# An attention kernel with a dense layer behind it: engines of the small operations from a table, q and k of the last five groups turned by DMA, the last output tile in three parts

## The chip, the core and the metric

The kernel runs on one core of one Trainium2 chip. A core has five engines that run side by side, each through its own queue in order: PE (TensorE, matrix products and transposes through an identity), DVE (VectorE), ACT (ScalarE), POOL (GpSimd) and SP (SyncE, which here issues every DMA). Sixteen DMA engines move the data. The metric is the device time in microseconds, from several runs of the same program; less is better.

## What is computed

Inputs are q, k and v of shape (8 batches, 8 heads, 576 tokens, 64), and two weights, 512x2048 and 2048x512. Cut to what matters:

```python
q_d, k_d, v_d = mean over 4 neighbouring tokens          # 144 tokens
out_d = softmax(q_d @ k_d.T / 8) @ v_d
out_up = np.repeat(out_d, 4, axis=2)
mask = np.abs(pos[:, None] - pos[None, :]) < 4
out_local = softmax(where(mask, q @ k.T / 8, -1e9)) @ v
x = (out_up + out_local) as (4608 tokens, 512)
h = x @ w_in
out = (h - np.tanh(h)) @ w_out
```

So attention is cheap (a band of seven tokens, and a pooled version), and the dense part is large: 4608 x 512 x 2048 twice.

## The kernel before

**An order planned ahead.** The body doesn't issue instructions; it hands operations to a small planner, `Program` (L16). Each operation names its engine, an estimated duration in ns, what it reads and writes, and a priority `pri` (a lower number goes first). `choice` (L56) gives several engines with a duration for each, and the planner takes the one that can start first. `order` (L62) plays the program through with these durations, a lag behind each engine (`LAT`) and an added margin `spare` (L244), which depends on the priority: from 120 on, and again from `LATER` on, steps that wait for another engine are planned later than they need be. The resulting order of each engine's queue is fixed; on the chip each instruction waits only for its own inputs.

**Units.** A pair `p` (0 to 31) is two heads of one batch; four pairs are a batch (NP = 4). A group `n` (0 to 15) is two pairs, the unit in which q and k are loaded. The dense part has 9 blocks of 512 tokens.

**q and k.** `load_qk(n)` (L344) loads q (i = 0) and k (i = 1) into `qkn`. `reorder(n, i)` (L450) casts and sorts them into `qr` (bf16), on the engines of `REORDER`: any of three for groups 0 and 1, from group 2 on DVE for q and POOL for k. `turn(n, i)` (L459) turns `qr`: nine transposes on PE (L479) into a PSUM bank, a copy that spreads the result into `qk` (L486; ACT or DVE in groups 0 and 1, ACT later), and two sums that pool four tokens into `qkd` (L496 and L501; DVE or POOL in groups 0 and 1, POOL later). A branch `n >= FI` that turns `qr` by a DMA transpose into v buffers 4 and 5 is in the code, but `FI` is 99 and there are 16 groups, so it doesn't run.

**v.** `load_v(p)` (L362) loads v into one of six buffers `vst`; `prep_v(p)` (L415) casts it into `vw` (POOL or ACT for the first four pairs, then POOL). The pooled v is made on PE by `pool_v` (L423, copied out by ACT) for groups 0 to 6, and from group 7 by a second load and sums on POOL (`load_v4`, `sum_v`).

**A pair.** `attention(p)` (L510): first scores s1 on PE (L533), exp on ACT (L568), mask on DVE (L572); then s2 (the last tile's scores and the pooled ones, L533 and L552), exps (L591, L594), mask (L598); then the outputs on PE (L609, L615), a reciprocal and the norm into `ln` on DVE (L624, L626). Up to pair 11 `ln` is turned on PE, the pooled rows are copied by ACT to `od` (L667), and DVE adds both into `xT` (L669). From pair 12 (`XOUT`) `ln` is turned by a DMA transpose that SP issues (L634), and DVE adds (L645). The loads of pair p wait until the DMA turn of pair p - 5 was issued (`AHEAD` = 5). From pair 12 (`MERGE`) s1 of the next pair is issued together with s2.

**The dense part.** `mm1(kb, fc)` (L679) does four matmuls (L692) into one of four PSUM banks `ps_hy`, tanh on ACT (L701) and the difference on DVE into `gT` (L704). `mm2(kb, i)` (L711) does the second product (L720), four matmuls at a time; after sixteen ACT copies the 128x512 tile to `y` (L731) and SP stores it (L734). All dense matmuls have priority 5000, so PE takes them when nothing of attention is ready; their ACT and DVE steps have -1. Blocks 2 to 8 are interleaved with the second product of the block before. Block `kb` needs x of every batch that its tokens lie in: blocks 0 to 6 end in batches 0 to 6, blocks 7 and 8 in batch 7.

**The start.** PE has nothing dense to do until batch 0 is through; the planner fills its gaps there with matmuls on a constant tile (L903). The weights are loaded and cast (L410) in the meantime.

**What sets the order around the change.** The main loop (L868) visits the pairs; in each it hands in the pooled v of a new group, the cast of v of pair p + 2, the pair's scores, and the reorders and turns of the coming group, before or after the pair's second half by `INNER`, `OUTER` and `EARLY`; then the loads of the next group. The planner keeps its own order by priority and readiness; the place in the loop decides which use of a shared buffer comes first.

Of the kernel before, what the change touches and what calls it, by code (L numbers as in the profile page):

```python
# [11 lines left out]
ALU = mybir.AluOpType  # L12
# [3 lines left out]
class Program:  # L16
# [10 lines left out]
    def __init__(self):  # L27
        self.ops = []
        self.alternatives = {}
        self.touch = []  # L30
        self.fresh = set()
        self.spare = lambda pri, eng, to: 0
        self.last_write = {}
        self.readers = {}

    def op(self, eng, ns, fn, reads=(), writes=(), pri=0):
        i = len(self.ops)
        deps = set()
        for key in reads:
            if key in self.last_write:  # L40
                deps.add(self.last_write[key])
        for key in writes:
            if key in self.last_write:
                deps.add(self.last_write[key])
            deps.update(self.readers.get(key, ()))
        for key in reads:
            self.readers.setdefault(key, set()).add(i)
        for key in writes:
            self.last_write[key] = i
            self.readers[key] = set()  # L50
        deps.discard(i)
        self.ops.append((eng, ns, fn, deps, pri))
        self.touch.append(set(reads) | set(writes))
        return i

# [99 lines left out]
def kernel(  # L155
# [9 lines left out]
    nc = tc.nc  # L165
# [83 lines left out]
    LATER = 180  # L249
# [59 lines left out]
    def slot_v(p):  # L309
        return p % 4 if p >= 2 * FI else p % NVST  # L310
# [4 lines left out]
    def load_v4(n):  # L315

        b, h0 = n // 2, 4 * (n % 2)
        base = v[b, h0]
        for i, (g0, m) in enumerate(((0, 128), (128, 16))):
            rows = bass.AP(tensor=base.tensor, offset=base.offset + 4 * D * g0,  # L320
                           ap=[[4 * D, m], [S * D, 4], [1, 4 * D]])
            to = v4[128 - m:128, i]
            load(650, lambda to=to, rows=rows: nc.sync.dma_start(out=to, in_=rows),
                 [("qkn", 2, i, y) for y in range(2)], (1800, 250)[i], -30,
                 [("fl", 2 * n - AHEAD)])

    def sum_v(n):

        w, pri = n % NVW, 20 * n - 1
        for i in range(2):  # L330
            pp = slice(96 * i, 128)
            t = v4[pp, i].rearrange("p h (a d) -> p h a d", d=D)
# [11 lines left out]
    def load_qk(n):  # L344

        b, h0, s = n // 2, 4 * (n % 2), slot_qk(n)
        for i, src in enumerate((q, k)):
            for y in range(2):
# [13 lines left out]
    def load_v(p):  # L362

        b, j, s = p // NP, p % NP, slot_v(p)
        t = vst[s]
        for i in range(2):
# [48 lines left out]
    def prep_v(p):  # L415
        s, w, jj = slot_v(p), (p // 2) % NVW, p % 2
        P.choice([(eng, ns, lambda fn=fn: fn(  # L417
            out=vw[w][:, 2 * jj:2 * jj + 2, :, 0:64], in_=vst[s]))
                  for eng, ns, fn in CAST_V[p >= NEARLY]],
# [3 lines left out]
    def pool_v(hb):  # L423

        w = hb % NVW
        pri = 20 * hb - 1
# [3 lines left out]
        def mm():  # L430
# [11 lines left out]
           reads=[key], writes=[("vd", w)], pri=pri)  # L442
# [7 lines left out]
    def reorder(n, i):  # L450
        s, sn = n % 2, slot_qk(n)
        dst = qr[s][:, i].rearrange("p a (x d) -> p x a d", d=D)
        srt = qkn[sn][:, i].rearrange("p x (a d) -> p x a d", d=D)
        P.choice([(eng, ns, lambda fn=fn: fn(out=dst, in_=srt))  # L454
                  for eng, ns, fn in REORDER[n >= 2][i]],
# [3 lines left out]
    def turn(n, i):  # L459

        s = n % 2
        ps, po, ts, ox = banks_of(2 * n + i)
        if n in (1, 2):
            ps, ts = po, ox
        pri, cold = 20 * n, (1.5 if n < 1 else 1.0)
        b16 = ps.rearrange("p n c -> p (n c)").bitcast(BF16)[:, 0:A6 * 128]
        if n >= FI:
            b16 = vst[4 + i].rearrange("p h t d -> p (h t d)").bitcast(BF16)[:, 0:A6 * 128]
# [16 lines left out]
        def copy(fn):  # L485
            fn(out=o.rearrange("p y (g a) -> p y g a", a=A6),  # L486
               in_=b16.rearrange("p (a g y) -> p y g a", a=A6, y=2))
        P.choice([(eng, ns, lambda fn=fn: copy(fn)) for eng, ns, fn in TURN[n >= 2]],
                 reads=ts, writes=[("qk", s, i)], pri=pri)


        four = o.rearrange("p y (g a) -> p y g a", a=4)
        adders = ADDERS[n >= 2]

        def add1(eng):
            eng.tensor_tensor(out=half, in0=four[:, :, :, 0:2],  # L496
                              in1=four[:, :, :, 2:4], op=ALU.add)

        def add2(eng):
            with nc.allow_low_precision("pooled q and k"):  # L500
                eng.tensor_tensor(out=qkd[s][:, i], in0=half[:, :, :, 0],  # L501
                                  in1=half[:, :, :, 1], op=ALU.add)
        P.choice([(name, n1, lambda eng=eng: add1(eng)) for name, n1, _, eng in adders],
                 reads=[("qk", s, i)], writes=["half"], pri=pri)
        P.choice([(name, n2, lambda eng=eng: add2(eng)) for name, _, n2, eng in adders],
                 reads=["half"], writes=[("qkd", s, i)], pri=pri)

    nexts = {}

    def attention(p):  # L510
# [6 lines left out]
        late = 25 if p < 2 else pri  # L517
# [36 lines left out]
        qks = [("qk", sq, i) for i in range(2)]  # L554
# [6 lines left out]
        qkds = [("qkd", sq, i) for i in range(2)]  # L561
        if p <= MERGE:
            op("PE", 420 * cold, s1, reads=qks, writes=ts, pri=pri)
# [6 lines left out]
           reads=ts, writes=[("E", se, 0)], pri=pri)  # L570
# [16 lines left out]
        else:  # L587
            op("PE", 380 * cold, s2, reads=qks + qkds, writes=ox if p >= MERGE else ts,
               pri=pri)
        sb = ox if p >= MERGE else ts  # L590
        op("ACT", 335, lambda: A.activation(  # L591
            out=e2v, in_=pb[:, :, 0:96], func=AF.Exp, scale=SCALE),
           reads=sb, writes=[("E", se, 1)], pri=pri)
        op("ACT", 655, lambda: A.activation(  # L594
            out=e3, in_=pb[:, :, 96:384], func=AF.Exp, scale=SCALE / 16.0),
           reads=sb, writes=[("E", se, 2)], pri=pri)
# [8 lines left out]
        def outs():  # L605
# [13 lines left out]
        P.fresh.add(len(P.ops))  # L619
        op("PE", 570 * cold, outs,  # L620
# [9 lines left out]
            op=ALU.mult), reads=ox + [("r", s)], writes=[("ln", sl)], pri=late)  # L630
# [28 lines left out]
        def back():  # L659
# [8 lines left out]
           reads=ox, writes=[("od", s)], pri=late)  # L668
# [4 lines left out]
           reads=ox + [("od", s)], writes=[("x", b, j)], pri=late)  # L673
# [5 lines left out]
    def mm1(kb, fc):  # L679
# [15 lines left out]
        for part in range(2):  # L695
# [4 lines left out]
               writes=[("hy", slot)] + old, pri=5000)  # L700
# [8 lines left out]
    yn = [0]  # L709

# [28 lines left out]
    def dense(kb):  # L739
# [13 lines left out]
        for i in range(16):  # L753
            if kb < NBLK:
                mm1(kb, i)
            mm2(kb - 1, i)
# [3 lines left out]
    XOUT, T_OUT, AHEAD = 12, 1600, 5  # L760
    MERGE, GV = 12, 7
    FI, T_IN, EARLY = 99, 2050, 12
    XADD = [("DVE", (800, 350), V)]
    ORDER, W_FIRST = "g0123", "0123g"
    INNER, OUTER = {4: [0], 5: [1]}, {3: [0, 1], 7: [0, 1]}
    W_LATE = [300, 1400, 0, 0]
    T_QK, T_V, T_W, W_PRI, NEARLY = 900, 780, 2750, 33, NP
# [3 lines left out]
              [("POOL", 790, GP.tensor_copy)]]  # L771
    any3 = [("DVE", 860, V.tensor_copy), ("ACT", 950, A.copy),
            ("POOL", 1350, GP.tensor_copy)]
    REORDER = [[any3, any3], [[("DVE", 1150, V.tensor_copy)], any3[2:3]]]
    TURN = [[("ACT", 1125, A.copy), ("DVE", 1250, V.tensor_copy)],
            [("ACT", 1125, A.copy)]]
    ADDERS = [[("DVE", 760, 440, V), ("POOL", 1190, 850, GP)],
              [("POOL", 1190, 880, GP)]]
# [6 lines left out]
    for i in range(2):  # L785
        def guards(i=i):
# [3 lines left out]
           writes=[("qk", i, a) for a in range(2)])  # L790
# [26 lines left out]
    for step in W_FIRST:  # L817
        if step == "g":
            load_qk(2)
            load_v(4)  # L820
# [47 lines left out]
    for p in range(NPAIR):  # L868
        n = p // 2
        if p % 2 == 0 and 1 < n < GV:  # L870
            pool_v(n)
        if p + 2 >= NP and p + 2 < NPAIR:
            prep_v(p + 2)
        if p >= 2:
            next(work[p])
        inner = INNER.get(p, [] if p < 2 * NP else [p % 2] if p < EARLY else
                          [0, 1] if p == EARLY else [1] if p % 2 == 0 else [])
        m = n + 1 + (p > EARLY)
        outer = OUTER.get(p, [0] if p > EARLY and p % 2 else [])
        for i in inner if n + 1 < NGRP else []:  # L880
            reorder(n + 1, i)
            turn(n + 1, i)
        next(work[p], None)
        for i in outer if m < NGRP else []:
            reorder(m, i)
            turn(m, i)
# [48 lines left out]
```

## Time and profile before

| | |
|---|---|
| median of 13 runs | 340.86 us (339.39 to 343.98) |
| the profiled execution: time | 340.86 us |
| its span, first to last instruction | 339.1 us |
| mean granted clock of TensorE | 0.995 |
| busy: DVE, ACT, POOL | 228.1, 199.8, 157.9 us |
| dense matmuls L692 and L720, each | 576 loads of weights |
| transposes of q and k, L479 | 288 loads of weights |
| DMA: bytes, mean rate | 57.51 MB, 170 GB/s |
| DMA turns of `ln` (L634) | 20; 3.1 us to landing, 1.25 us to issue |

Times are from one profiled execution; L12 is line 12 of the kernel. "Busy" for PE contains pipelined matmuls whose ends are modelled, so rates are read from start to start. Where a queue sat idle, the profile names what ended the wait; idle time of an engine that isn't the bottleneck costs nothing. The granted clock is the share of full speed at which TensorE was let run in a stretch, and the DMA share is the mean busy share of the sixteen DMA engines. It can pass 1, since packets overlap.

The first matmuls of block 0 run at 26.1 and 26.7 us, and without a break from 29.5 us on. The last x is written at 265.3 us.

### The profile page before, as it was taken

What the parts mean: (1) busy time and instruction counts of PE and PEld (TensorE: products, weight loads), DVE (VectorE), ACT (ScalarE), POOL (GpSimd) and SP (SyncE); (2) the same over time, 40 slices, a digit from 0 to 9 for tenths busy, and PEclk for the clock granted to TensorE, in tenths of its full rate; (3) what the DMA queues carried; (4) which work ended last, traced back from release to release, by engine and by line L of the source; (5) the groups of instructions that cost most, each with busy time, mean ns of one, the idle gap of its engine ahead of it and who ended that gap; (6) DMA issues with size and microseconds to landing.
All of it is one profiled execution on the core that took longest, in us unless ns stands there. A gap on an engine that the chain in (4) does not pass through costs nothing.

```text
span 339.1 us, 6802 instructions
## 1 busy us (share of the span) xinstructions
PE 322.7 (95%) x2578; PEld 168.4 (50%) x2624; DVE 228.1 (67%) x369; ACT 199.8 (59%) x334; POOL 157.9 (47%) x178
## 2 busy tenths in 40 slices
PE   6786999999999999999999999999999999999995
PEld 2462554655565555555554545454444444444442
DVE  4986697568977877887689988986666433343300
ACT  1564887678967865676575757576544434444411
POOL 7743786496884449687458666862000000000000
PEclk9997999999999999999999999999999999999999
DMA  6999999999712598895798599962212000100021
GB/s 221 259 386 286 284 366 307 292 293 303 210 42 18 136 239 234 219 244 154 193 239 226 151 245 160 261 141 76 73 43 76 31 31 33 62 31 33 31 90 64
DMA packets 84749, 57.51 MB, mean 170 GB/s; under 512 B 62638, under 2 KB 67822, under 8 KB 84718
## 3 DMA queue, kind: packets, MB, share of 16 engines
q1 hardware_dynamic: 84718, 57.09, 61.9%
q8 instruction: 20, 0.33, 0.4%
q14 instruction: 11, 0.09, 0.1%
HBM read 43.05 MB, written 9.44 MB: 155 GB/s over the span
## 4 chain that ended last, share of the span: by engine, by line
PE 83%; DVE 7%; issue 3%; SPq 2%; DMA 2%; POOL 1%; ACT 1%; ACTq 0%; POOLq 0%; DVEq 0%
PE ps_hy L720 35%; PE ps_hy L692 33%; PE ps_ts L479 4%; PE ps_ts L533 3%; PE ps_ox L609 3%; PE ps_ox L615 2%; DMA vst<-in_v_dram 2%; SPq L357 1%; DVE gT L704 1%; DVE ln L626 1%; DVE xT L645 1%; PE ps_ox L432 1%; DVE E L572 1%; DVE xT L669 1%; DVE qr L454 1%
## 5 line engine op out<-in xcount | busy, mean ns | idle before, releaser
L692 PE MATMUL ps_hy<-xT,w_in_sb 128*128 128x512 bf16 x547 | 143.4, 383 | 3.8 <-DVE xT L669 1.8
L720 PE MATMUL ps_hy<-w_out_sb,gT 128*128 128x512 bf16 x560 | 140.7, 379 | 1.2 <-issue 0.3
L704 DVE TENSOR_TENSOR gT<-ps_hy,uy 128x512 bf16<-128x512 f32 x144 | 95.9, 686 | 62.5 <-ACT uy L701 60.4
L701 ACT ACTIVATE uy<-ps_hy 128x512 f32<-128x512 f32 x144 | 83.4, 602 | 69.3 <-PE ps_hy L692 64.1
L720 PEld LDWEIGHTS <-gT 128*128 128x128 bf16 x576 | 54.1, 98 | 61.4
L692 PEld LDWEIGHTS <-w_in_sb 128*128 128x128 bf16 x576 | 53.2, 98 | 60.7 <-issue 5.3
L496 POOL TENSOR_TENSOR half<-qk 128x576 f32<-128x576 bf16 x28 | 34.8, 1243 | 29.8 <-ACT qk L486 21.6
L486 ACT COPY qk<-ps_ts 128x1152 bf16<-128x1152 bf16 x26 | 29.3, 1127 | 10.4 <-PE ps_ts L479 8.9
L626 DVE TENSOR_TENSOR ln<-ps_ox,r 128x896 bf16<-128x896 f32 x30 | 32.7, 1089 | 0.8
L731 ACT COPY uy<-ps_hy 128x512 f32<-128x512 f32 x36 | 21.2, 590 | 18.3 <-PE ps_hy L720 17.6
L568 ACT ACTIVATE E<-ps_ts 128x960 bf16<-128x960 f32 x30 | 29.2, 977 | 3.7 <-PE ps_ts L533 2.9
L454 POOL CAST qr<-qkn 128x1152 bf16<-128x1152 f32 x17 | 21.9, 1286 | 18.8 <-DMA qkn<-in_k_dram 18.4
L334 POOL TENSOR_TENSOR qkn<-qkn 128x512 f32<-128x512 f32 (+1 forms) x18 | 24.2, 1346 | 7.9 <-DMA qkn<-in_v_dram 7.1
L572 DVE TENSOR_TENSOR E<-E,mask 128x960 bf16<-128x960 bf16 x28 | 24.3, 867 | 5.0 <-ACT E L568 5.0
L417 POOL CAST vw<-vst 128x640 bf16<-128x640 f32 x32 | 25.0, 794 | 4.5 <-DMA vst<-in_v_dram 2.0
L645 DVE TENSOR_TENSOR xT<-lnT 128x480 bf16<-128x480 bf16 (+1 forms) x40 | 24.0, 617 | 0.0
L501 POOL TENSOR_TENSOR qkd<-half 128x288 bf16<-128x288 f32 x29 | 22.7, 784 | 2.7 <-DVE half L496 1.3
L479 PEld LDWEIGHTS <-qr 128*128 128x128 bf16 x288 | 18.5, 99 | 9.7 <-DVE qr L454 3.7
L479 PE MATMUL ps_ts<-ident,qr 128*128 128x128 bf16 x252 | 19.2, 222 | 2.0 <-DVE qr L454 1.9
L598 DVE TENSOR_TENSOR E<-E,mask 128x192 bf16<-128x192 bf16 x28 | 12.9, 461 | 10.5 <-ACT E L591 10.4
L609 PE MATMUL ps_ox<-vw,E 128*128 128x65 bf16 x300 | 18.2, 194 | 0.3 <-DVE E L598 0.3
L609 PEld LDWEIGHTS <-E 128*128 128x128 bf16 x300 | 15.3, 98 | 6.3 <-DVE E L598 0.4
(90 smaller groups left out, 251.8 us busy)
## 6 DMA issues: line engine op xcount, KB each, us to landing
vst<-in_v_dram SPq DMA_DIRECT2D x62, 160.0 KB, 5.2
qkn<-in_q_dram SPq DMA_DIRECT2D x32, 288.0 KB, 4.0
qkn<-in_k_dram SPq DMA_DIRECT2D x32, 288.0 KB, 4.9
out_dram<-uy SPq DMA_DIRECT2D x36, 256.0 KB, 2.1
qkn<-in_v_dram SPq DMA_DIRECT2D x9, 512.0 KB, 5.0
gT<-in_moe_w_in_dram SPq DMA_DIRECT2D x4, 1024.0 KB, 9.0
xT<-in_moe_w_out_dram SPq DMA_DIRECT2D x8, 256.0 KB, 4.1
gT<-in_moe_w_out_dram SPq DMA_DIRECT2D x2, 1024.0 KB, 9.6
```

The costliest lines, as they stand in the source:

```text
L479: T.transpose(b16[:, 128 * a:128 * a + 128], qr[s][:, i, a, :], ident)
L486: fn(out=o.rearrange("p y (g a) -> p y g a", a=A6), in_=b16.rearrange("p (a g y) -> p y g a", a=A6, y=2))
L496: eng.tensor_tensor(out=half, in0=four[:, :, :, 0:2], in1=four[:, :, :, 2:4], op=ALU.add)
L568: op("ACT", 980, lambda: A.activation(out=e1, in_=ps[:, :, 0:480], func=AF.Exp, scale=SCALE), reads=ts, writes=[("E", se, 0)], pri=pri)
L572: op("DVE", 900, lambda: V.tensor_tensor(out=e1, in0=e1, in1=mask[:, 0:480].unsqueeze(1).to_broadcast([128, 2, 480]), op=ALU.mult), reads= ...
L609: T.matmul(po[:, hh, 65 * t:65 * t + 65], E[se][:, c:c + 128], vw[w][:, 2 * jj + hh, t, :], start=True, stop=True)
L626: op("DVE", 1090, lambda: V.tensor_tensor(out=ln[sl].rearrange("p n (h d) -> p h n d", d=D), in0=blocks[:, :, :, 0:64], in1=r[s].unsqueeze ...
L645: up=up: eng.tensor_tensor(out=xo[:, QW * t0:QW * t0 + nt * n].rearrange("p (t g a) -> p t g a", t=nt, a=4), in0=lnT[sl][:, t0:t0 + nt, 0: ...
L692: T.matmul(ps_hy[slot], w_in_sb[:, dc, fc * 128:(fc + 1) * 128], xT[dc][:, kb * 512:kb * 512 + 512], start=(dc == 0), stop=(dc == N_DC - 1))
L701: op("ACT", 490, lambda: A.activation(out=u[us], in_=ps_hy[slot], func=AF.Tanh), reads=[("hy", slot)], writes=[("u", us)], pri=-1)
L704: op("DVE", 620, lambda: V.tensor_tensor(out=gT[g][:, fc, :], in0=ps_hy[slot], in1=u[us], op=ALU.subtract), reads=[("hy", slot), ("u", us) ...
L720: T.matmul(ps_hy[slot], gT[g][:, fc, ts * 128:ts * 128 + 128], w_out_sb[:, fc, :], start=(fc == 0), stop=(fc == N_FF - 1))
```

## The change

Five things, with one table or setting each:

1. For groups 0 to 5 and pairs 0 to 11 the engine of each step is given by a table with an entry for each: the cast of v (`CV`), the reorder (`RE`), the copy of the turned tile (`TU`) and the sums (`AD`). Some copies and sums are split into two halves, one for each pair of the group (`TS`, `AS`), which may go to different engines. From group 6 on the engines are as before.
2. Groups 11 to 15 (`FI` = 11) are turned by the DMA transpose of the existing branch; the copy then reads SBUF. v of pairs from 22 on has four buffers in place of six, as two receive the turned tiles.
3. The last output tile (`last_tile`) is made in columns 0-256, 256-384 and 384-512, each with its own matmuls, copy (ACT, ACT, DVE) and store.
4. Places and priorities: which pair's loop turns a group stands in (`PLACE`), when pooled v is handed in (`PV`), a priority of -2 for some steps of pairs 4 to 11 (`URG`), other priorities for the last steps of pairs 0 to 3 (`LATE`), which groups' turns use the other PSUM bank (`TB`).
5. `AHEAD` is 6 in place of 5, and `LATER` 160 in place of 180.

The rest (`put`, `has`) are assertions at build time and issue nothing. `SPARE`, `MERGE`, `XOUT` and the planner are as before.

```diff
@@ slot of v
-        return p % 4 if p >= 2 * FI else p % NVST
+        if p < 2 * FI:
+            return p % NVST
+        return (p - 2 * FI + 2 * (FI % 3 == 1)) % 4
...
@@ prep_v
-                  for eng, ns, fn in CAST_V[p >= NEARLY]],
+                  for eng, ns, fn in CAST_V[CV.get(p, 1)]],
...
@@ reorder
-                  for eng, ns, fn in REORDER[n >= 2][i]],
+                  for eng, ns, fn in REORDER[RE.get((n, i), 3 + i)]],
...
@@ turn
-        if n in (1, 2):
+        if (n, i) in TB:
             ps, ts = po, ox
...
+        both = [(slice(0, 2), (0, 1))]
+        each = [(slice(y, y + 1), (y,)) for y in range(2)]
+        parted = TS.get((n, i), 0)
+        for k, (ys, yy) in enumerate(each if parted else both):
+            table = (TURN_H[parted - 1][k] if parted else
+                     TURN[3 if n >= FI else TU.get((n, i), 1)])
+            P.choice([(eng, ns, lambda fn=fn, ys=ys: copy(fn, ys)) for eng, ns, fn in table],
+                     reads=ts, writes=[("qk", s, i, y) for y in yy],
+                     pri=URG.get("turn", {}).get(n, pri))
...
+    def last_tile(kb, ts):
...
+        for c0, c1, engs in ((0, 256, "A"), (256, 384, "A"), (384, 512, "V")):
...
+            for e in range(4):
+                fcs = range(4 * e, 4 * e + 4)
+                op("PE", (c1 - c0) * 1.7, lambda fcs=fcs, mm=mm: mm(fcs),
...
+            fn = A.copy if engs == "A" else V.tensor_copy
...
@@ dense
-            mm2(kb - 1, i)
+            if kb < NBLK or i < 12:
+                mm2(kb - 1, i)
+        if kb == NBLK:
+            last_tile(kb - 1, 3)
@@ settings
-    LATER = 180
+    LATER = 160
...
-    XOUT, T_OUT, AHEAD = 12, 1600, 5
+    XOUT, T_OUT, AHEAD = 12, 1600, 6
+    P_A, LATE = 5000, {0: 26, 1: 5, 2: 25, 3: 25}
-    FI, T_IN, EARLY = 99, 2050, 12
+    FI, T_IN = 11, 2050
...
-    INNER, OUTER = {4: [0], 5: [1]}, {3: [0, 1], 7: [0, 1]}
+    TB = {(1, 0), (1, 1), (2, 0), (3, 0)}
+    PV = {2: -1, 3: 0, 4: 1, 5: 0, 6: 0}
+    PLACE = {2: (2, 4), 3: (1, 3), 4: (4, 4), 5: (0, 2), 6: (2, 3), 7: (1, 1), 8: (0, 3)}
...
+    CV = {0: 0, 1: 0, 2: 3, 3: 1, 4: 1, 5: 0, 6: 0, 7: 3, 8: 1, 9: 0, 10: 2, 11: 1}
...
+    RE = {(0, 0): 4, (0, 1): 4, (1, 0): 4, (1, 1): 4, (2, 0): 1, (2, 1): 0, (3, 0): 3, (3,
+          1): 4, (4, 0): 3, (4, 1): 4, (5, 0): 1, (5, 1): 1}
     TURN = [[("ACT", 1125, A.copy), ("DVE", 1250, V.tensor_copy)],
-            [("ACT", 1125, A.copy)]]
+            [("ACT", 1125, A.copy)], [("DVE", 1250, V.tensor_copy)],
+            [("ACT", 2210, A.copy)]]
+    TU = {(0, 0): 0, (0, 1): 0, (1, 0): 1, (1, 1): 0, (2, 0): 0, (2, 1): 0, (3, 0): 0, (3,
+          1): 0, (4, 0): 2, (4, 1): 1, (5, 0): 2, (5, 1): 0}
...
+    TS, AS = {(0, 0): 1, (1, 1): 3, (4, 0): 3}, {(0, 1): 3, (1, 1): 3}
+    URG = {'e1': {4: -2, 5: -2, 6: -2, 7: -2}, 'od': {4: -2, 5: -2, 6: -2, 7: -2}, 'norm':
+          {8: -2, 9: -2, 10: -2, 11: -2}, 'add': {4: -2, 5: -2, 6: -2, 7: -2}, 'turn': {4:
+          -2, 5: -2}}
...
+    AD = {(0, 0): 0, (0, 1): 1, (1, 0): 0, (1, 1): 2, (2, 0): 1, (2, 1): 0, (3, 0): 0, (3,
+          1): 0, (4, 0): 1, (4, 1): 0, (5, 0): 0, (5, 1): 2}
```

In `CV`, `RE` and `TU` the numbers pick a row: of the v casts 0 is POOL or ACT, 1 POOL, 2 ACT, 3 DVE; of the reorders 0 is any of three, 1 DVE, 2 ACT, 3 DVE and 4 POOL with the durations of the later groups; of the copies 0 is ACT or DVE, 1 ACT, 2 DVE, 3 ACT from SBUF. In `AD` 0 is DVE or POOL, 1 POOL, 2 DVE.

## The prediction

> **What bounds the kernel.** First, the busy shares and the chain of waits (the work that ended last, followed back from the end):
>
> ```profile
> PE 322.7 (95%) x2578; PEld 168.4 (50%) x2624; DVE 228.1 (67%) x369; ACT 199.8 (59%) x334; POOL 157.9 (47%) x178
> PE 83%; DVE 7%; issue 3%; SPq 2%; DMA 2%; POOL 1%; ACT 1%; ACTq 0%; POOLq 0%; DVEq 0%
> ```
>
> PE carries the chain. A busy PE need not be an efficient one, so I look at what it does. The dense part is 1152 matmuls (9 blocks, 64 on L692 and 64 on L720), and a run of eight takes 1.73 us from start to start, 0.216 each: 248.8 us. Attention fills the gaps. So the end is: when the dense stream begins, plus all PE work after that, plus PE's idle time, plus the tail behind the last matmul. I take the stages in that order, by the table of busy time per stretch (columns: us, then busy us and instructions of PE, PEld, DVE, ACT, POOL, granted clock, DMA share, GB/s):
>
> ```profile
> 28.00:29.00 1.00, 0.28 (x6) 0.18 (x4) 0.32 (x1) 0.51 (x2) 0.20 (x1) 1.00 0.99 373
> 31.00:32.00 1.00, 1.00 (x4) 0.37 (x3) 0.94 (x3) 0.60 (x1) 0.00 (x0) 0.50 0.94 169
> ...
> 160.00:180.00 20.00, 19.75 (x176) 10.59 (x178) 15.20 (x27) 12.80 (x21) 10.75 (x12) 1.00 0.84 210
> 180.00:200.00 20.00, 19.33 (x169) 10.19 (x172) 18.66 (x28) 13.18 (x22) 15.20 (x16) 1.00 0.74 189
> 200.00:222.00 22.00, 21.84 (x180) 11.24 (x182) 19.50 (x28) 13.98 (x24) 14.96 (x15) 1.00 1.01 228
> 222.00:244.00 22.00, 21.84 (x185) 11.28 (x185) 16.55 (x29) 13.84 (x23) 7.90 (x8) 1.00 0.33 73
> ```
>
> Before 29.5 us PE waits for x; DVE, the engine that makes x, is the full one there (8.8 of 10 us in both 10-20 and 20-30). From 29.5 on PE hardly stops: 3.3 us idle in all of 30-240, 0.4 behind that. The clock is at half from 30 to 33, which costs some 1.7 us (15 matmuls in 4.9 us, not 3.2).
>
> **The supply of x is as tight as PE.** Blocks 7 and 8 run L692 and L720 in turn, 32 steps of 1.73 us, 55.3 us in all; L692 ends at 320.6, so block 7 starts at about 265.3. The timeline says when the last x is there (first line), and how far apart the pairs' second scores (s2) stand behind the last turn:
>
> ```profile
> 265.07 0.25 DVE L645 TENSOR_TENSOR xT<-lnT 128x96 bf16<-128x96 bf16 x1
> ...
> 235.66 0.21 PE L533 MATMUL ps_ox<-qk 64*128 64x96 bf16 x2
> ...
> 244.16 0.21 PE L533 MATMUL ps_ox<-qk 64*128 64x96 bf16 x2
> ...
> 253.29 0.22 PE L533 MATMUL ps_ox<-qk 64*128 64x96 bf16 x2
> ```
>
> Batch 7 becomes ready in the very microsecond in which PE wants it. Time taken off PE counts only if attention comes earlier too.
>
> **q and k of groups 11-15 turned by DMA.** Ten turns of nine transposes leave PE. One costs, from its start to that of what follows it:
>
> ```profile
> 208.80 0.67 PE L479 MATMUL ps_ts<-ident,qr 128*128 128x128 bf16 x9
> 209.30 1.89 PE L720 MATMUL ps_hy<-w_out_sb,gT 128*128 128x512 bf16 x8
> ```
>
> 0.50 us; ten are 5.0, on the path (the 0.67 is a modelled end that overlaps its successor). They come back elsewhere:
>
> - DMA. The nearest row is the turn of ln (128x896, 229 KB), issued at 243-245 with nothing else moving: shares of 0.62 and 0.57 in two stretches of 1 us, 1.2 us of all engines. Scaled by 1152/896 a turn of q or k is 1.5, ten are 15. The Trainium skill (DMA: Bandwidth & Descriptors, Latency and other measured facts) gives DMA transposes 261 GB/s where the middle dimension isn't contiguous: 1.1 each for 295 KB, 11 in all. The row decides. From 162 to 222 DMA is busy for 0.90 x 60 = 54 us; with 15 it is 69, 9 us more than fit. Cover: the last turn is at 225.5 and its user is the score of pair 30 at 243.9, or 238.9 when PE runs 5 us ahead: 13 us. So hidden, with 4 us to spare. If the landing time (3.1 us of the ln turns) were the cost, 31 us: the third rival.
> - SP. An issue took 1.25 us, so 12.5 us in a queue that also issues loads, ln turns and outputs, and each stands behind the reorder it waits for: DVE for q, POOL for k. Behind it in the queue stand the next loads. AHEAD 6 instead of 5 lets those go one pair (about 8 us) sooner, more than a wait for one reorder (1.3 us). Nothing taken.
> - v buffers fall from six to four behind pair 22. A load then waits for the cast of the pair four before; that cast stands two pairs ahead of its own pair, so it is done when the load may go by AHEAD anyway. Nothing.
> - ACT. The copy that spreads the turned tile now reads SBUF. The row that it has from PSUM:
>
> ```profile
> L486 ACT COPY qk<-ps_ts 128x1152 bf16<-128x1152 bf16 x26 | 29.3, 1127 | 10.4 <-PE ps_ts L479 8.9
> ```
>
> The copy reads with a step of 128 elements (256 bytes). The skill's page SBUF — State Buffer (Door 1: The DMA port swizzle) says that each access that crosses into another 16-byte line pays a penalty; the diff's table prices the copy at 2.21. No row here shows it. By the row ten copies cost nothing new; by the rule and the table some 11 us more. ACT has 40.0 busy in 160-222, so 51 of 62 us: it fits, but tanh and exp sometimes stand behind a 2.2 us copy. I take the dearer.
>
> New waits: the fullest engine of before, DVE in 180-200 (93%), goes with 0.67 us of idle PE per 20 us. Were ACT to do the same over 62 us, 2.1 us, against 1.08 idle there now: +1.0. Bounds: 0 (ps_hy has four slots) and 3.3, as much as all the idle of 30-240 again.
>
> **The tables for batches 0-2.** From 30 to 120 PE is idle for 1.6 us in all, so there they can hardly bring time, only let x come sooner or later. Before 29.5 they can. On DVE they remove the reorder of q 0 (0.76), half of two copies (1.36 each: 1.36) and perhaps the copy of k 0 (1.35); they add one v cast (estimate 0.55, from 0.42 for 512 columns on DVE). Net 1.6 to 2.9 less, in a chain where DVE is full but for the 0.6 us before 19.4, when it waited for the first output. Against it: all four reorders stand on POOL (1.15 each), where the mask of 1.90 lies at 5.3; k 0 can come 1.15 later. Bounds +1.2 and -2.9; I take -1.5, as the v casts (12.84 at the earliest, when v landed) hold part of the chain. The cold clock I leave: the gap ahead of 29.5 gets shorter, not closed.
>
> **The last tile in parts.** Behind the last matmul:
>
> ```profile
> 335.53 0.59 ACT L731 COPY uy<-ps_hy 128x512 f32<-128x512 f32 x1 [2.87 <-PE ps_hy L720]
> 336.15 0.33 SPq L734 DMA_DIRECT2D out_dram<-uy  x1
> ```
>
> The copy of 128 columns costs a quarter of the elements: an estimate of 0.25 from the 128x96 row above, 0.34 less. The last transfer is a quarter too: 262 KB took 0.7 of a microsecond (share 0.70 in 245-246), so some 0.5 less. PE: 32 matmuls of 128 columns at 0.056 (nine in 0.50) and 16 of 256 at 0.108, 3.5 us for 3.46. Sum -0.8; bounds 0 (fixed cost of a DMA is all) and -1.2.
>
> **Sum.** -5.0 + 1.0 - 1.5 - 0.8 = -6.3. The profiled execution's span was 339.1 and its time 340.86, the median too, so 1.76 lies around the span: 332.8 + 1.76 = **334.6**.
>
> **Rivals.**
>
> - Supply sets the end (attention no faster). For it: pairs behind the last turn stand 8.5 and 9.1 us apart with no turn between, as far as those with turns (187.5 to 195.9, 8.4), so the turns do not pace the chain of a pair. Against: loads go out earlier, the score bank is held by no turn (1.8 us and more each) from group 11 on, and what batches 0-2 gain is lead. Then only front and tail count: -2.3, **338.6**.
> - More goes: the clock stays up at 30-33 (1.7) and half of the idle PE of 30-240 (1.6) goes: 334.6 - 3.3 = **331.3**. For it: the gap before the stream may fall under what drops the clock; against: PE still waits for DVE there.
> - DMA becomes the bound (slower). Place: 160-240, where the share is 0.74 to 1.01 already. At 3.1 us a turn, 54 + 31 = 85 us of transfers in 60, 25 late, 13 covered: 12 us late, **346.6**. It makes the kernel slower than before from 2.63 us a turn (6 free + 13 covered + 7.3, by ten). Against: the share at 243-245 says 1.2 for a tile nearly as large.
>
> That the change does not do what it says shows as L479 with 288 loads of weights, not 198; nothing in the diff speaks for it.
>
> **Chances and range.** Forecast 0.54, supply 0.20, more 0.12, DMA 0.14. What a measurement can tell from no change is 0.3%, 1.0 us. Faster: the first three, less 0.05 of the supply case near 340: 0.81. Same 0.05, slower 0.14. The forecast's own range, from the new waits (0 to 3.3), the front (1.2 to -2.9) and the tail, each seldom at its end, is 332 to 337.5; to leave out two in ten it takes in the supply case and part of the better one: 330.8 to 339.3.
>
> **What would show it.** Right: L479 at 198 weight loads; span about 333; last x near 259; start of the steady L692 near 28. ACT's copies from SBUF near 2.2 us, PE idle in 160-222 near 2. Wrong: last x still at 264-265 and PE idle or out of dense work before it (supply); qk copies waiting for the DMA turns with shares of 1 past 222 (DMA); a first L692 stream at 29.5 or later (front).

## The result and the profile after

The changed kernel takes 337.81 us in the median of its 11 runs (335.19 to 339.51), against 340.92 for the kernel before, beside it and in the runs shown earlier (48 in all). The ratio is 0.9905, interval 0.9878 to 0.9932: faster by 3.1 us, where 6.3 were forecast. The profiled execution took 337.05, its span was 335.3, so 3.8 below the profiled one of before. One later execution of `turns_only`, at a granted clock of 0.558 from end to end, took 553.42 us and is left out everywhere; six other executions lie over 1.5% above the fastest of their kernel and stay in, as they move no median in the table below by more than 0.3 us.

The page of the changed kernel (busy us, share of the span, instructions; then groups with the mean ns of one):

```profile
PE 319.3 (95%) x2522; PEld 165.5 (49%) x2565; DVE 239.4 (71%) x385; ACT 207.7 (62%) x337; POOL 150.7 (45%) x168
...
L514 ACT COPY qk<-ps_ts 128x1152 bf16<-128x1152 bf16 (+1 forms) x15 | 16.0, 1064 | 13.9 <-DVE qk L514 8.1
...
L514 ACT COPY qk<-vst 128x1152 bf16<-128x1152 bf16 x10 | 22.2, 2221 | 1.6 <-POOL half L518 1.6
```

PE is as full as before, with 56 instructions fewer (90 transposes less, 32 small matmuls more, a few records missing). The ten copies that now read SBUF (from `vst`) take 2.22 us each where the same copy from PSUM takes 1.13: the table in the diff was right, and the dearer end was the one to take.

The busy time by stretch, in the columns of the prediction's table. The first four rows are the stretches shown there for before. The last four are two earlier stretches, each of the changed kernel and then of before:

```profile
160.00:180.00 20.00, 19.63 (x153) 9.60 (x156) 16.47 (x25) 15.28 (x23) 11.92 (x13) 1.00 1.05 235
180.00:200.00 20.00, 19.89 (x153) 9.65 (x148) 15.88 (x27) 17.58 (x25) 14.45 (x16) 1.00 1.19 234
200.00:222.00 22.00, 21.84 (x185) 10.98 (x186) 20.17 (x32) 16.19 (x25) 13.96 (x14) 1.00 1.08 230
222.00:244.00 22.00, 21.84 (x170) 10.81 (x169) 16.64 (x29) 15.40 (x23) 8.27 (x8) 1.00 0.42 107
...
40.00:70.00 30.00, 28.11 (x274) 15.81 (x277) 26.90 (x40) 20.66 (x36) 18.84 (x22) 1.00 1.00 308
40.00:70.00 30.00, 29.38 (x295) 16.57 (x298) 23.41 (x36) 22.56 (x39) 20.68 (x25) 1.00 1.04 318
70.00:120.00 50.00, 48.97 (x489) 27.50 (x497) 43.99 (x68) 38.55 (x66) 31.82 (x33) 1.00 0.68 174
70.00:120.00 50.00, 49.07 (x482) 27.67 (x489) 40.47 (x65) 39.61 (x66) 34.73 (x37) 1.00 0.60 164
```

From 160 to 222 PE is idle for 0.64 us (1.08 before), although ACT rose from 40.0 to 49.1 us and the DMA share from 0.87 to 1.11. The late half, where the large gain was to come from, does somewhat better than forecast. The early half doesn't: in 40-70 PE is idle for 1.9 us where it was 0.6. The timeline of PE says when the dense stream begins and when PE gets the last x of batch 2, first in the changed kernel and then before (in brackets the idle time before an entry, and what ended it):

```profile
29.26 6.75 PE L739 MATMUL ps_hy<-xT,w_in_sb 128*128 128x512 bf16 x23 [1.21 <-DVE xT L715]
...
102.96 0.72 PE L453 MATMUL ps_ox<-vw,pick 128*128 128x256 bf16 x5 [0.34 <-DVE xT L715]
...
29.49 5.08 PE L692 MATMUL ps_hy<-xT,w_in_sb 128*128 128x512 bf16 x15 [1.21 <-DVE xT L669]
...
101.03 0.72 PE L432 MATMUL ps_ox<-vw,pick 128*128 128x256 bf16 x5 [0.34 <-DVE xT L669]
```

The stream begins 0.2 us sooner than before, not 1.5, and x of batch 2 is complete at 102.9, where it was 101.0. From there to the last matmul it is 102.9 to 332.4, 229.5 us, against 101.0 to 335.45, 234.45 us: 4.95 less. That this meets the 5.0 of the turns is partly chance, for the other tables and settings are in it too; `fi99` below takes the turns off alone. So this pair of profiles reads: 1.9 us lost in front of batch 3, 5.0 won behind it, and at the end

```profile
328.69 3.70 PE L769 MATMUL ps_hy<-w_out_sb,gT 128*128 128x256 bf16 x48
...
332.48 0.29 DVE L777 COPY uy<-ps_hy 128x128 f32<-128x128 f32 x1 [13.49 <-PE ps_hy L769]
```

2.9 us of tail behind the last matmul instead of 3.65. Sum: 1.9 - 5.0 - 0.7 = -3.8.

**Equal clocks.** A profile is one execution, and the spans of one and the same kernel differ by up to 5 us. Each run lists its mean granted clock, and the spread goes with it. In the profiles the clock falls to a half for 3.4 us or a multiple of it: from 30.0 to 33.4 us before, and from 8.7 to 12.1 and 29.2 to 32.6 in the changed kernel. I call 3.4 us of this a cold stretch. Each takes 0.005 off the mean (half of 3.4, in 337), so a mean of 0.99 stands for two. Among 78 runs of the kernel before, the median span is 337.9 with no cold stretch (0.998 or more, 27 runs), 338.7 with one (21), 339.9 with two (0.988 to 0.992, 11) and 340.9 with three (19): about 1 us for each, less than the 1.7 that the prediction worked out for the one at 30.

So the table gives, beside medians, the median span at full clock (0.998 or more) and with two cold stretches, each with its number of runs. The changed kernel was run again beside the last experiments and has 18 runs in all, of which 14 have two. Like with like the change is worth 4.3 us (full clock) or 3.9 us (two cold stretches); the medians show 3.1, because it is seldom at full clock.

| kernel | median time, us | span at full clock (runs) | with two cold stretches (runs) |
|---|---|---|---|
| before (78 runs) | 340.62 | 337.9 (27) | 339.9 (11) |
| changed (18) | 337.47 | 333.6 (2) | 336.0 (14) |
| `fi99`: changed, no DMA turns | 341.57 | 338.5 (4) | 340.6 (5) |
| `whole`: changed, last tile whole | 338.34 | 334.8 (4) | 337.6 (6) |
| `tables_old`: changed, old tables | 337.74 | 335.1 (3) | none |
| `turns_only`, `turns_2`: before, DMA turns | 338.42 | 335.6 (7) | 336.6 (4) |
| `front_new`: before, new tables of groups 0, 1 | 345.37 | 340.4 (2) | 342.4 (1) |
| `front_old`: changed, those tables old | 339.73 | 336.0 (2) | 338.3 (6) |
| `ahead5`: changed, AHEAD 5 | 339.79 | 334.7 (2) | 338.2 (6) |
| `old_lead`: `tables_old`, LATER 999 | 337.67 | 334.8 (3) | 335.8 (2) |
| `warm`, `warm_2`: changed, six fillers | 335.42 | 333.2 (6) | 338.2 (2) |

Runs of one kernel at full clock still spread by 1 to 3 us, so differences under 1 us say little, and a median of two or three runs says little more. Behind 40 us and up to the last matmul the clock is full in every profile but that of the execution left out, so stretches of two profiles can be compared there directly.

### The profile page after: what moved, and what is told of

It reads as the page before. It is cut to its first block, busy times and chain, and to the rows that moved or that the text cites. A ratio compares the mean times of both kernels' runs of the same rounds, so it can differ in the third digit from the quotient of the medians.

```text
span 335.3 us, 6713 instructions
## 1 busy us (share of the span) xinstructions
PE 319.3 (95%) x2522; PEld 165.5 (49%) x2565; DVE 239.4 (71%) x385; ACT 207.7 (62%) x337; POOL 150.7 (45%) x168
## 4 chain that ended last, share of the span: by engine, by line
PE 77%; SPq 7%; DVE 6%; DMA 6%; issue 2%; ACT 1%; POOL 0%; POOLq 0%; DVEq 0%; ACTq 0%
PE ps_hy L739 32%; PE ps_hy L794 32%; DMA qkn<-in_k_dram 5%; SPq L398 3%; PE ps_ox L652 3%; PE ps_ts L572 2%; SPq L372 2%; PE ps_ox L658 2%; PE ps_ts L505 2%; DMA xT<-in_moe_w_out_dram 1%; DVE gT L751 1%; PE ps_hy L769 1%; DVE ln L671 1%; SPq L417 1%; SPq L410 1%
## 5 line engine op out<-in xcount | busy, mean ns | idle before, releaser
L739 PE MATMUL ps_hy<-xT,w_in_sb 128*128 128x512 bf16 x549 | 143.1, 383 | 4.3 <-DVE xT L715 2.2
L794 PE MATMUL ps_hy<-w_out_sb,gT 128*128 128x512 bf16 x545 | 137.5, 379 | 0.8 <-issue 0.2
L739 PEld LDWEIGHTS <-w_in_sb 128*128 128x128 bf16 x576 | 53.5, 98 | 62.5 <-issue 5.2
L794 PEld LDWEIGHTS <-gT 128*128 128x128 bf16 x560 | 52.6, 98 | 59.1
L518 POOL TENSOR_TENSOR half<-qk 128x576 f32<-128x576 bf16 x26 | 31.8, 1221 | 50.1 <-ACT qk L514 44.5
L805 ACT COPY uy<-ps_hy 128x512 f32<-128x512 f32 x35 | 20.9, 597 | 14.9 <-PE ps_hy L794 13.2
L348 POOL TENSOR_TENSOR qkn<-qkn 128x512 f32<-128x512 f32 (+1 forms) x18 | 24.9, 1385 | 7.2 <-DMA qkn<-in_v_dram 5.6
L691 DVE TENSOR_TENSOR xT<-lnT 128x480 bf16<-128x480 bf16 (+1 forms) x40 | 26.5, 676 | 0.0
L477 POOL CAST qr<-qkn 128x1152 bf16<-128x1152 f32 x17 | 21.1, 1243 | 8.6 <-DMA qkn<-in_k_dram 8.0
L514 ACT COPY qk<-ps_ts 128x1152 bf16<-128x1152 bf16 (+1 forms) x15 | 16.0, 1064 | 13.9 <-DVE qk L514 8.1
L514 ACT COPY qk<-vst 128x1152 bf16<-128x1152 bf16 x10 | 22.2, 2221 | 1.6 <-POOL half L518 1.6
L634 ACT ACTIVATE E<-ps_ox 128x192 bf16<-128x192 f32 x20 | 6.7, 334 | 18.6 <-PE ps_ox L591 17.4
L572 PEld LDWEIGHTS <-qk 64*128 64x128 bf16 x320 | 9.3, 95 | 16.2 <-issue 13.8
```

The costliest lines, as they stand in the source:

```text
L348: op("POOL", 1330, lambda t=t: GP.tensor_tensor(out=t[:, :, 0:2], in0=t[:, :, 0:2], in1=t[:, :, 2:4], op=ALU.add), writes=keys, pri=pri)
L514: fn(out=o[:, ys].rearrange("p y (g a) -> p y g a", a=A6), in_=b16.rearrange("p (a g y) -> p y g a", a=A6, y=2)[:, ys])
L518: eng.tensor_tensor(out=half[:, ys], in0=four[:, ys, :, 0:2], in1=four[:, ys, :, 2:4], op=ALU.add)
L691: up=up: eng.tensor_tensor(out=xo[:, QW * t0:QW * t0 + nt * n].rearrange("p (t g a) -> p t g a", t=nt, a=4), in0=lnT[sl][:, t0:t0 + nt, 0: ...
L739: T.matmul(ps_hy[slot], w_in_sb[:, dc, fc * 128:(fc + 1) * 128], xT[dc][:, kb * 512:kb * 512 + 512], start=(dc == 0), stop=(dc == N_DC - 1))
L794: T.matmul(ps_hy[slot], gT[g][:, fc, ts * 128:ts * 128 + 128], w_out_sb[:, fc, :], start=(fc == 0), stop=(fc == N_FF - 1))
```

## The experiments

Each part of the change can be taken off alone. The old tables are put back as values of the new ones; together with FI 99, AHEAD 5, LATER 180 and the whole tile that is the kernel before, instruction for instruction, so no part of the change is left out. Theory A and theory B in the expectations are two readings of the first result, told in the first of them.

### The parts alone

`tables_old`:

```diff
-    CV = {0: 0, 1: 0, 2: 3, ...}
+    CV = {p: 0 for p in range(4)}
-    RE, TU, AD = (a table of groups 0-5 each)
+    RE, TU, AD = 0 for groups 0 and 1
-    TS, AS, URG = {(0, 0): 1, ...}, ...
+    TS, AS, URG = {}, {}, {}
-    PV, PLACE, TB, LATE = (as changed)
+    PV, PLACE, TB, LATE = (as before)
```

> The changed kernel with every table and place of batches 0-2 as before (engines of casts, reorders, copies and sums, no halves, no priorities of -2); DMA turns, last tile, AHEAD 6 and LATER 160 stay. Theory A (the tables cost some 1.9 us, since x of batch 2 is there at 102.9 instead of 101.0; the DMA turns give their 5.0 us in full): 5.7 us below before, about 335.2, x of batch 2 near 101, PE idle in 40-70 back to 0.6 us from 1.9. Theory B (the tables do nothing, the DMA turns give only half because x of batch 7 comes no sooner): as the changed kernel, 337.5, x of batch 7 at 264-265.

Neither. 337.74 is the changed kernel's time. The early loss is gone, as theory A has it: x of batch 2 comes at 100.5 (in a profile without a cold stretch), and PE is idle for 1.0 us in 40-70. But from there to the last matmul it takes 231.7 us, where the changed kernel takes 229.5; its PE is idle for 2.1 us in 200-330 (0.7 before, 1.0 changed). Whether the new tables pay once the DMA turns are in is not settled: at full clock the old ones are 1.5 us slower (3 runs against 2), in the medians 0.3, and `old_lead` below, with the old tables too, is level with the changed kernel at two cold stretches.

`fi99`:

```diff
-    FI, T_IN = 11, 2050
+    FI, T_IN = 99, 2050
```

> The changed kernel with no group turned by DMA (FI 99), everything else as changed. Theory A: 5.0 us above the changed kernel, about 1.2 above before, 342. Theory B: 2.5 above the changed kernel, about 340.

341.57, ratio to before 1.0014 (0.9979 to 1.0049). The profile of `fi99` is the cleanest measure of the turns, for it has its two cold stretches within half a microsecond of where the changed kernel has them. PE gets the last x of batch 2 at the same time; here are that point and the last matmuls, first of `fi99`, then of the changed kernel:

```profile
102.89 0.72 PE L453 MATMUL ps_ox<-vw,pick 128*128 128x256 bf16 x5 [0.34 <-DVE xT L715]
...
333.77 2.93 PE L769 MATMUL ps_hy<-w_out_sb,gT 128*128 128x256 bf16 x41
...
330.83 1.56 PE L769 MATMUL ps_hy<-w_out_sb,gT 128*128 128x128 bf16 x25
```

336.7 against 332.4: 4.3 us behind batch 2. At full clock it is 4.9, with two cold stretches 4.6: theory A's term. (The 4.1 between the medians mixes clocks, and most runs of `fi99` have 2.0 us or more around the span, where the others have 1.7.) The rest of the change on its own gains nothing, though the tile in it is worth about 1.

`whole`:

```diff
-            if kb < NBLK or i < 12:
-                mm2(kb - 1, i)
-        if kb == NBLK:
-            last_tile(kb - 1, 3)
+            mm2(kb - 1, i)
```

> The changed kernel with the last tile in one piece as before. Both theories: 0.75 us above the changed kernel, with 3.65 us from the last matmul to the end of the span instead of 2.9.

338.34, 0.9 above the changed kernel in the median, 1.2 at full clock; in its profile 4.0 us stand behind the last matmul, 1.1 more than in the changed one. The forecast for the tile was 0.8. That profile also says that the late x of batch 2 is not the clock's doing: it has one cold stretch (29.4 to 32.8 us), as before has, and is 2.2 us behind before all the same:

```profile
103.22 0.72 PE L453 MATMUL ps_ox<-vw,pick 128*128 128x256 bf16 x5 [0.34 <-DVE xT L715]
```

`turns_only`, and `turns_2`, the same kernel once more:

```diff
 (the kernel before)
-    FI, T_IN, EARLY = 99, 2050, 12
+    FI, T_IN, EARLY = 11, 2050, 12
```

> The kernel before with FI 11 alone (AHEAD 5, LATER 180, last tile whole). Theory A: 5.0 us below before, 336. Theory B: 2.3 below before, 338.6. If AHEAD 6 is what lets the turns pay: 1 to 2 us slower than tables_old after the 0.75 of the tile, with DMA-fed copies late and PE idle in 160-222 above 2 us.

> The kernel before with FI 11 alone, once more, for a profile at a normal clock. Theory D (old tables and AHEAD 5 leave PE short of work once the turns are gone): span 2.4 us below before at full clock, idle PE from 120 on 2 us above the 1.7 of before, and copies of turned tiles or dense matmuls of a new block named as late. Rival: no more idle PE than before and the 2.4 us was noise of three runs; then it is 4.5 to 5 below.

338.42 in 21 runs, 335.6 at full clock: 2.3 below before (3.3 with two cold stretches, and 3.7 by the profiles behind batch 2: 230.8 us against 234.5). The turns are worth 2.3 to 3.7 us in the kernel before and 4.3 to 4.9 in the changed one. The profile of `turns_2` shows a part of the difference. Its row of 200-240, then that of before, and ACT and PE around the last turned tiles:

```profile
200.00:240.00 40.00, 38.21 (x307) 18.99 (x311) 31.34 (x51) 32.92 (x47) 24.59 (x26) 1.00 0.85 205
200.00:240.00 40.00, 39.68 (x341) 20.83 (x346) 32.48 (x51) 26.23 (x43) 22.86 (x22) 1.00 0.73 162
```

```profile
230.86 4.29 ACT L514 COPY qk<-vst 128x1152 bf16<-128x1152 bf16 x2
235.02 0.61 ACT L805 COPY uy<-ps_hy 128x512 f32<-128x512 f32 x1
235.49 0.63 ACT L748 ACTIVATE uy<-ps_hy 128x512 f32<-128x512 f32 x1
```

```profile
235.20 0.38 PE L572 MATMUL ps_ts<-qk 64*128 64x120 bf16 x8 [0.58 <-ACT qk L514]
236.90 1.45 PE L739 MATMUL ps_hy<-xT,w_in_sb 128*128 128x512 bf16 x6 [0.18 <-DVE gT L751]
```

PE is idle for 1.8 us in 200-240, 0.3 before. Two copies of 2.2 us stand one behind the other on ACT; a dense output copy and a tanh wait behind them for four microseconds, and PE waits for the scores and then for the free bank. In the changed kernel the ten copies are 3.5 us or more apart from start to start, and PE's idle time in 200-240 is 0.3. From 120 on the idle PE of `turns_2` is 3.4 us against 2.1 before (to 330): 1.3 us of what is missing are seen as waits; the rest could not be placed. Copies that meet are not the whole cause. In `tables_old` they are 3.5 us or more apart too, and yet its PE is idle for 3.4 us from 120 to 330, 1.5 of it in three waits for output copies (L805), at 137, 203 and 267.

### Is it the supply of x?

`old_lead`:

```diff
 (tables_old)
-    LATER = 160
+    LATER = 999
```

> The old tables with DMA turns, last tile and AHEAD 6 (as in tables_old, whose span at full clock was 335.1, with 2.1 us of idle PE in 200-330), and the second step of margin off (LATER 999), so that late pairs are planned closer together. Theory D (with old tables the DMA turns are held back by the supply of x): x of batch 7 earlier by 2 us or more, idle PE in 200-330 under 1 us, span at full clock near 333.6. Rival (PE's idle there comes from waits that the margin prevents): as slow or slower, more idle PE.

x of batch 7 came at 263.3, where it was 264.1 in `tables_old`: 0.8 us sooner, not the 2 that were wanted. Idle PE in 200-330 went from 2.1 to 1.6 us, but rose from 1.3 to 1.8 in 120-200, and the time is the same (334.8 at full clock, three runs from 333.3 to 336.5). So this run hardly tests theory D; `turns_2` speaks more against it, for its x of batch 7 is the earliest of all (262.5) and its PE is no less idle.

`ahead5`:

```diff
-    XOUT, T_OUT, AHEAD = 12, 1600, 6
+    XOUT, T_OUT, AHEAD = 12, 1600, 5
```

> The changed kernel with AHEAD 5. If the earlier loads carry the DMA turns: copies of turned tiles late, PE idle in 160-240 from 0.8 to above 1.8 us, 1 us or more slower (334.6 at full clock and above). If they don't matter: within 0.5 us of the changed kernel.

339.79: 2.3 us slower in the median, 1.1 at full clock (2 runs), 2.2 with two cold stretches (6 runs). So AHEAD 6 is worth 1 to 2 us here, where the prediction had it at nothing. Its profile, full in clock from 35 us on, shows a part of the way. Behind batch 2 it takes 231.1 us (229.5), and two of the copies meet on ACT, as in `turns_2`. The row is to be read beside the changed kernel's 21.84 of 22:

```profile
222.00:244.00 22.00, 20.98 (x161) 10.18 (x163) 17.00 (x27) 18.34 (x26) 12.57 (x14) 1.00 0.76 185
...
237.30 4.29 ACT L514 COPY qk<-vst 128x1152 bf16<-128x1152 bf16 x2
...
243.35 1.89 PE L739 MATMUL ps_hy<-xT,w_in_sb 128*128 128x512 bf16 x8 [0.61 <-DVE gT L751]
```

PE is idle for 1.0 us there, 0.2 in the changed kernel. Whether AHEAD 6 would pay as much without DMA turns, no run says; with the old tables it does not show (231.7 us behind batch 2 in `tables_old` with AHEAD 6 and LATER 160, 230.8 in `turns_2` with 5 and 180).

### The front

`front_old` (the changed kernel, with the tables of groups 0 and 1, pairs 0-3 and LATE as before):

> The changed kernel with the tables of groups 0 and 1 and pairs 0-3 (and their priorities) as before; those of groups 2-5 as changed. If the new front is what shortens PE's idle start: stream later by 0.2 to 1.5 us and as much slower at full clock (333.8 to 335.1). If it is neutral and the later tables carry the lead: 333.6 at full clock. PE idle in 40-70 stays at 1.9 us if the tables of groups 2-5 make it, and falls to 0.6 if those of groups 0 and 1 do.

339.73, 2.3 us above the changed kernel, 2.4 at full clock. Its profile stood at three cold stretches, up to 37 us; what lies behind is at full clock:

```profile
40.00:70.00 30.00, 29.42 (x273) 16.28 (x276) 25.42 (x39) 22.29 (x39) 18.85 (x23) 1.00 0.99 292
70.00:120.00 50.00, 44.95 (x459) 25.58 (x467) 42.15 (x62) 33.43 (x60) 30.35 (x31) 1.00 0.61 160
```

PE's idle time in 40-70 falls to 0.6 us, so the tables of groups 0 and 1 make the 1.9 of the changed kernel; but without them 5.1 us are idle in 70-120. `front_new` is its mirror, the same tables put into the kernel before:

```diff
 (the kernel before, by its tables)
-    P_A, LATE = 5000, {0: 25, 1: 25}
+    P_A, LATE = 5000, {0: 26, 1: 5, 2: 25, 3: 25}
-    CV = {p: 0 for p in range(4)}
+    CV = {0: 0, 1: 0, 2: 3, 3: 1}
-    RE = 0 for groups 0 and 1
+    RE = 4 for groups 0 and 1
-    TU, AD = 0 for groups 0 and 1; TS, AS = {}, {}
+    TU = {..., (1, 0): 1, ...}; AD = {..., (0, 1): 1, ..., (1, 1): 2}
+    TS, AS = {(0, 0): 1, (1, 1): 3}, {(0, 1): 3, (1, 1): 3}
```

> The kernel before with the changed tables of groups 0 and 1 and pairs 0-3 alone (no DMA turns, no other table, AHEAD 5, LATER 180, last tile whole). The prediction's term: 1.5 us below before at equal clock (336.6 of span at full clock, before 338.1). Rival from the profile of the changed kernel, whose stream starts 0.2 us sooner and whose x of batch 2 is 1.9 us later: 0 to 2 us slower than before.

345.37, ratio 1.0122 (1.0088 to 1.0155): 2.5 us slower at full clock, 3.3 with three cold stretches, and more in the median as 9 of its 12 runs have three. The forecast term had the wrong sign. The stream starts at 29.65 in its profile (29.49 before), so the front itself is no shorter; and one stretch further PE runs out of work. Its row of 70-120:

```profile
70.00:120.00 50.00, 47.40 (x469) 27.05 (x477) 40.75 (x62) 38.31 (x66) 35.23 (x37) 1.00 0.62 161
```

2.6 us idle against 0.9 before (49.07 busy). Pairs 4 to 11 were placed for the old front. With the changed tables of groups 2-5 the same front is worth 2.3 us instead. The old front with the new tables of groups 2-5 and the new front with the old ones both lose, in the same stretch: these tables can't be priced one by one.

Why the front isn't shorter is in the changed kernel's timeline of DVE and ACT, where the first copy of q is split in halves:

```profile
7.21 0.76 DVE L514 COPY qk<-ps_ts 128x576 bf16<-128x576 bf16 x1 [3.91 <-PE ps_ts L505]
8.00 0.64 ACT L514 COPY qk<-ps_ts 128x576 bf16<-128x576 bf16 x1 [5.92 <-DVE qk L514]
```

ACT had been idle for 5.9 us and starts 0.03 after DVE ends, released by DVE. The halves run one behind the other: 7.21 to 8.64, 1.43 us, against 1.36 for the one copy of before. Nor is the first reorder shorter: POOL takes 1.14 for q 0 (DVE took 0.76), and only then the mask.

### The clock

`warm`, and `warm_2`, the same kernel once more:

```diff
                 fill[i] = (name, int(0.75 * room / slow))
+            more = min(self.start[i] for i in range(len(self.ops))
+                       if ("hy", 3) in self.touch[i])
+            two = {name: banks[name] for name in ("ts", "ox")}
+            for i, name, room in self.idle(order, two, more):
+                if self.start[i] >= until:
+                    fill[i] = (name, int(0.75 * room / 230))
```

It fills PE's planned gaps behind the first dense matmul with six matmuls on the constant tile, one and then five ahead of the steady stream.

> The changed kernel with six matmuls on the constant tile more in PE's gaps between the first dense matmul and the steady stream. Theory C (the cold clock at 28-33 us costs the changed kernel the 1.5 us between its median's gain and that of its runs at full clock): fewer runs below a clock of 0.995, median near 335.8, spans near 333.6. Rival (the clock falls for what PE does earlier, or the fillers hold up the stream): median 337.8 or more, clocks as before.

> The changed kernel once more, beside the others. If the change is worth 4.4 us at equal clock and the 3.1 us between the medians is the luck of ten low-clock runs in twelve: with a third of the runs at full clock the median falls to 336-337. If it loses full clock more often than before: again few runs at 0.998 or above, and a median of 337.5 or more.

> The changed kernel with the six matmuls on the constant tile, once more. If they keep the clock up: more than half of the runs at 0.998 or above again and a median 1 us or more below after_2. If four in six was luck: a third, and the median of after_2.

`after_2`: 337.24, none of 6 runs at full clock, so the few in the first twelve were not bad luck. `warm`: 335.20, ratio 0.9878 (0.9818 to 0.9938); `warm_2`: 335.62, 0.9844 (0.9798 to 0.9890). At full clock are 4 of 6 runs of `warm`, but 2 of 6 of `warm_2`: by this count alone the expectation's "luck" came, while the median, 1.6 us below `after_2`, is the other outcome. At 0.993 or more (one cold stretch at most) are 9 of the 12, 3 of 18 of the changed kernel and 48 of 78 of before. Equal in clock it is no faster than the changed kernel (333.2 and 333.6 at full clock, 338.2 and 336.0 with two cold stretches): what the fillers bring is the clock, 2.0 us in the median. That makes it the fastest kernel of this study, 4 to 5 us below before. Whether it is the new front that makes cold stretches likelier is not shown: kernels with it have 6 of 12 (`fi99`), 5 of 11 (`whole`), 4 of 12 (`ahead5`) and 2 of 12 (`front_new`) at 0.993 or more, those with the old one 5 of 6 (`tables_old`) and 12 of 21 (the DMA turns alone), but also 4 of 12 (`front_old`) and 5 of 12 (`old_lead`).

The changed kernel's profile (the clock is the third number from the end: 0.90 of full speed in 10-20, where before had 1.00) shows a second cold stretch, earlier than the one at 30:

```profile
10.00:20.00 10.00, 8.82 (x106) 5.76 (x105) 8.88 (x16) 6.40 (x10) 5.22 (x6) 0.90 1.13 289
...
30.00:33.30 3.30, 3.30 (x11) 1.23 (x10) 1.68 (x3) 1.42 (x3) 0.87 (x1) 0.61 0.96 196
```

The Trainium skill (TensorE: Matmul & The Clock Gate, Part 1: The HAM clock gate) has the activity watched in a free-running window, and warns that the same kernel differs from run to run with where in the window it starts. The runs agree so far: one and the same program has none to three cold stretches, and a few fillers shift the odds. Which gap brings a stretch on, no run here shows.

## Why the prediction was right, and where it wasn't

The measured 337.8 lies in the range and the direction was right, but the gain is half of the forecast. The forecast's own range ended at 337.5; the number is inside only because the range took in the supply case, which did not come about. That is luck in part. By its steps, at equal clock:

- **Turns off PE, -5.0.** Held in the main, given the rest: 4.3 between the profiles of `fi99` and the changed kernel, 4.9 at full clock. In the kernel before they bring only 2.3 to 3.7.
- **New waits, +1.0.** ACT's 51 of 62 us came as 49.1, the copy at 2.22; the waits did not come in the changed kernel (0.64 us of idle PE in 160-222, not 2.1). In `turns_2` they did: +1.5 in 200-240.
- **DMA hidden, 0.** Held. A turn cost more than 1.5, and more than the 1.1 that the prediction estimated from the skill's page: with 8 turns issued in 160-222 the share is 1.11 instead of 0.85 in `fi99`, 16 us, 2.0 each. They landed 4.7 us after their issue in the median (3.3 to 5.9), and SP took 1.6 us to issue one, not 1.25. The last copy of a turned tile ended at 235.7, before the scores of pair 30 at 244.2.
- **AHEAD 6, 0.** Mis-sized: it brings 1.1 to 2.3 us by `ahead5`.
- **Last tile, -0.8.** -0.75 between the profiles of before and after, -1.1 between those of `whole` and after, -0.9 to -1.6 in the runs.
- **Tables of batches 0-2, -1.5.** This is the term that failed. The tables together with AHEAD and LATER, without DMA turns, cost some 1.8 us (`fi99` 338.5 against 337.9, with a tile worth 1.2 in it; 2.3 with two cold stretches). The sum of work taken off DVE was no price: the halves ran in turn, not side by side, and the stream started 0.2 us sooner. "They can hardly bring time" for 30 to 120 missed the other side: they could lose it, and did, 1.9 us by batch 2.
- **The cold clock, left.** It got likelier: some 1 us of the medians (3.9 to 4.3 at equal clock, 3.1 in the medians), which the fillers win back.

At full clock, then: -4.9 for the turns, -1.2 for the tile, +1.8 for the rest, -4.3 in all (with two cold stretches -4.6, -1.6, +2.3 and -3.9). The signs named ahead came in part: L505, the transposes, has 198 loads of weights, and the copies take 2.22 us; but the stream starts at 29.26, not 28, and the last x is there at 264.5, not 259.

That last miss touches the prediction's second thought, that PE's time counts only if x comes earlier too. Its reading, that batch 7 becomes ready in the microsecond in which PE wants it, was wrong: it counted back to a start of block 7 at 265.3. The first matmuls of block 7, before and changed, are these (the 449th of the 576 loads of weights of L692 and of L739 belongs to each):

```profile
267.09 1.89 PE L692 MATMUL ps_hy<-xT,w_in_sb 128*128 128x512 bf16 x7
...
263.94 1.03 PE L739 MATMUL ps_hy<-xT,w_in_sb 128*128 128x512 bf16 x4
```

So before, x (265.3) was 1.8 us ahead of its use. In the changed kernel block 7 starts 3.1 us sooner and x comes only 0.8 us sooner, half a microsecond behind the start, as the first half of a product needs only the first two pairs; PE does not wait for it. The supply rival was not the mechanism, though its 338.6 is nearer to the result than the forecast. In an order fixed ahead x follows PE's queue as much as PE follows x, so the end of x against the start of a block says little.

## What to carry to other kernels

Work taken off the engine that is the bound is worth what the order of the other engines lets it be: the same ten DMA turns brought 4.3 to 4.9 us in one order and 2.3 to 3.7 in another. In two of the slower orders the long copies that replace the work meet on ACT and PE waits behind them; a third loses as much with its copies apart, so spacing alone is not shown to be enough. Don't price a reassigned operation by the busy time that it takes off an engine; see whether its parts really run side by side, and what was placed for the old order behind it. And compare runs at equal clock before reading a few microseconds, then ask whether the change made the cold stretch likelier.

## What was not expected of the hardware

- The same 128x1152 bf16 copy on ACT, with a step of 256 bytes, takes 1.13 us from PSUM and 2.22 from SBUF.
- The clock falls to a half in stretches of 3.4 us in the first 37 us, none to three in executions of the same program, and each costs about 1 us of the span.
- Six matmuls on constant data, ahead of the dense stream, moved the share of runs with a mean clock of 0.993 or more from 3 of 18 to 9 of 12, and the median by 2.0 us.
